# Pooled attention and a routed expert layer on one core: the next unit's kind is read during the first layer, the transposes' compares stand ahead of their waits, and the second expert's weights begin after the first unit's first layer

## The chip, the core and the metric

The kernel runs on one core of a Trainium2 chip. The metric is the device time of one execution in microseconds (us); lower is better. Engines are named as in the profile: PE is the matrix engine, PEld its weight loads, DVE the vector engine, ACT the scalar engine, POOL the gather and scatter engine, SP the engine that issues the weights' transfers. Each has a sequencer of its own that runs register loads, compares, branches and semaphore waits in program order and hands the other instructions to its engine. A "q" behind an engine's name (PEq, PEldq) is that sequencer.

## The reference, cut to what matters

```python
def reference(q, k, v, w_skip, w_gate, w1, w2):       # 8 x 8 heads, 576 tokens, 64 wide
    # attention: k and v averaged over 8 tokens, softmax(q k^T / 8) v
    x = attention(q, k, v)                            # 4608 tokens x 512
    out = x.copy()
    do = (x @ w_skip) > 0                             # tokens that get an expert
    xc = x[do]
    e_idx = argmax(xc @ w_gate); gate = softmax(xc @ w_gate)[e_idx]
    for e in range(8):
        m = e_idx == e
        y[m] = gate[m] * (relu(xc[m] @ w1[e]) @ w2[e])   # 512 -> 1024 -> 512
    out[do] = xc + y
```

## The kernel before, in words

The attention is written out flat and fills the first 165 us or so; the tokens' routes are computed beside it. From 184.4 us on runs the part that the change touches, `experts`: a loop whose trip count and kinds come from the data.

**Units.** The tokens of each expert are cut into units of up to three tiles of 128 rows, called places 0, 1 and 2. `nti` holds for each unit its kind (how many places, how wide the last one is), and `ends` (0: the expert goes on, 1 or 2: this is its last unit, 2 with a short last tile), and the count of units. Each engine runs its own copy of the loop over units (`units`, a `Fori`) and keeps `kind`, `ends` and `after` (the last unit's `ends`) in registers; at the end of a pass it loads the next unit's two values from `nti` (L1114, L1115).

**PE, in a unit.** `first`: 8 blocks f of 12 matmuls each (x, split in a high and a low part, by w1, split alike), into three PSUM tiles in turn; `by_width` chooses one of five copies of it by the unit's width (compares and branches at L1091). From f = 3 on it waits for `lo`, by which DVE tells that block f - 3 is evacuated. Then `second` for places 0 and 1 (24 matmuls each), `tx` (the next unit's rows, which POOL has gathered, are transposed, 4 matmuls a place), then place 2, as `second` or, where `ends` is 2, `second_short` (16 matmuls). Place 2 and place 0 share a PSUM tile: `P(t, "psf0")` waits until DVE has taken place 0's result out of it. At the head of `first` PE waits for `x` (the rows, transposed and split by ACT and DVE).

**ACT and DVE, in a unit.** For each block f ACT writes the high part of the hidden layer (L1355) and DVE the low part (L1413). After an `ends` unit they also split the next expert's weights: the four chunks of w2 within the first layer (at f = 1, 3, 5, 7), and behind the first layer of an `ends` unit the four chunks of the next w1 (ACT L1341, DVE L1390). Then DVE adds places 0 and 1 to their rows (L1398), makes the low part of the next rows (L1385, `x`), adds place 2 (L1398, or L1404 and L1409 for a short one), and its sequencer loads the next unit's values.

**Weights.** An expert's w1 and w2 come in 8 chunks of 512 KB into 8 staging buffers, issued by SP in order (L1149). The second expert's 8 chunks wait for the semaphore `first`, which PE raises for each unit and SP waits for once; each chunk of a later expert waits until DVE has split the chunk before it in its buffer. Each engine's program is itself brought in by transfers: the profile's queue named "instruction".

**POOL** scatters each place's results to the output when `ob0` to `ob2` are raised, gathers the rows of the unit after the next, and raises `land0` to `land2` as they land.

Of the kernel before, what the change touches and what calls it, by code (L numbers as in the profile page):

```python
# [44 lines left out]
UNITS = MAXU + 2  # L45
# [19 lines left out]
TWO = 1  # L65
# [992 lines left out]
    return got  # L1058


def registers(e, nti):
    regs = [e.alloc_register(n) for n in ("tot", "kind", "ends", "after")]
    e.reg_mov(regs[3], 0)
    yield regs
    for r, i in zip(regs, (2 * UNITS, 0, UNITS)):
        e.reg_load(r, nti[0:1, i:i + 1])
        yield regs


def experts(tc, nc, out, w1, w2, whi, wlo, slot, gate, nti, kinds_a, steps, near, bufs, mb, ident, psum, upper):  # L1070
# [5 lines left out]
    with tc.tile_critical(no_gpsimd_drain=True):  # L1076
# [4 lines left out]
        def P(e, n, by=1):  # L1081
            e.wait_ge(sem[n], by).then_inc(sem[n], -by)  # L1082

        def V(e, n, by=1):
            e.sem_inc(sem[n], by)
# [17 lines left out]
            return (lambda: e.snap(off, min_val=0, max_val=3 * RW),  # L1103
                    lambda: e.reg_alu(off, off, 3 * RW, ALU.bitwise_xor))

        def units(e, regs, body):

            tot, kind, ends, after = regs
            n = e.snap(tot, min_val=1, max_val=MAXU)
            with e.Fori(0, n) as u:  # L1110
                body(u, e.snap(kind, min_val=0, max_val=TWO + 4), e.snap(ends, min_val=0, max_val=2),
                     e.snap(after, min_val=0, max_val=2), n - u)
                e.reg_mov(after, ends)
                e.reg_load(kind, nti[0:1, bass.ds(u + 1, 1)])  # L1114
                e.reg_load(ends, nti[0:1, bass.ds(u + UNITS + 1, 1)])  # L1115

        def by_width(e, kind, go, marks=None):

# [18 lines left out]
        with nc.Block(no_gpsimd_drain=True) as blk:  # L1137
# [81 lines left out]
            def _(t):  # L1219
                at, turn = parity(t, 1)  # L1220
                
                def tx(u):

                    o, after = at(), held[3]
                    t.reg_load(after, nti[0:1, bass.ds(u + 1, 1)])
                    three = t.snap(after, min_val=0, max_val=TWO + 4)
                    for i in range(3):
                        P(t, f"land{i}")
                    for unit, this in ((0, o < 1), (1, o > 0)):
                        def place(i, n):  # L1230
                            for k in range(4):
                                m = t.transpose(psD[i][:, k * 128:k * 128 + 128],
                                                ring[:, 3 * unit + i, k * 128:k * 128 + 128], ident)
                            m.then_inc(sem["pe"], n)

                        with t.If(this):
                            with t.If(three > TWO):
                                place(0, 1)
                                place(1, 1)
                            with t.If(three < TWO + 1):  # L1240
                                place(1, 2)
                            place(2, 1)
                    turn()

                def first(xs):

                    P(t, "x")
                    V(t, "first")
                    for f in range(8):
                        if f > 2:  # L1250
                            P(t, "lo")
                        ps, w = psL[f % 3][:, xs], slice(f * 128, f * 128 + 128)
                        for k in range(4):
                            t.matmul(ps, whi[0][:, k, w], xhi[:, k, xs], start=(k == 0), stop=False)  # L1254
                            t.matmul(ps, whi[0][:, k, w], xlo[:, k, xs], start=False, stop=False)  # L1255
                            last = t.matmul(ps, wlo[0][:, k, w], xhi[:, k, xs], start=False, stop=(k == 3))  # L1256
                        last.then_inc(sem["pe"], 1)
# [20 lines left out]
                        last = t.matmul(ps, hlo[:, k, sl], whi[1][:, k, :], start=False, stop=(k == 7))  # L1278
                    last.then_inc(sem["l2"], 1)

                def unit(u, kind, ends, _, left):
                    by_width(t, kind, first, marks)
                    with t.If(kind > TWO):
                        second(0, True)
                        second(1, False)
                    with t.If(kind < TWO + 1):
                        with t.If(kind > TWO - 1):
                            second(1, True)
                    with t.If(left > 1):
                        tx(u)  # L1290
                    with t.If(kind < TWO):
                        for _ in range(3):
                            P(t, "lo")
                    P(t, "psf0")
                    with t.If(ends < 2):
                        second(2, False)
                    with t.If(ends > 1):
                        second_short()

                assert len(steps) == SPARE  # L1300
                loads = registers(t, nti)
                held = next(loads)
                marks = {}

# [11 lines left out]
                for n, (_, _, f) in enumerate(steps):  # L1316
# [8 lines left out]
                    if n in BETWEEN:  # L1325
# [2 lines left out]
                        for k in range(4):  # L1328
                            m = t.transpose(psD[i][:, k * 128:k * 128 + 128], ring[:, i, k * 128:k * 128 + 128], ident)
                        m.then_inc(sem["pe"], 1)  # L1330
                units(t, held, unit)

            def half(f):

                return 4 + f // 2 if f % 2 else None

            @blk.scalar
            def _(a):
                def split(c):
                    P(a, f"wd{c}", 16)  # L1340
                    a.activation(chunk_of(whi, c), chunk_view(stage[c], c), AF.Copy).then_inc(sem["whi"], 1)  # L1341

                def x_high(i):
                    P(a, "pe")
                    a.activation(xhi[:, :, i * 128:i * 128 + 128], psD[i].rearrange("p (k n) -> p k n", k=4),  # L1345
                                 AF.Copy).then_inc(sem["act"], 1)

                def unit(u, kind, ends, after, left):
                    def parts(xs):
                        for f in range(8):  # L1350
                            if f % 2:
                                with a.If(after > 0):
                                    split(half(f))
                            P(a, "pe")
                            a.activation(hhi[:, f, xs], psL[f % 3][:, xs], AF.Relu).then_inc(sem["act"], 1)  # L1355

                    by_width(a, kind, parts)
                    with a.If(left > 1):
                        with a.If(ends > 0):
                            for c in range(4):  # L1360
# [12 lines left out]
            def _(v):  # L1373
# [34 lines left out]
                    v.engine_nop().then_inc(sem["psf0"], 1)  # L1408
                    v.scalar_tensor_tensor(x, upper, rf[0:64, bass.ds(o + (2 * RW + D), 1)], x, ALU.mult, ALU.add).then_inc(sem["ob2"], 1)  # L1409

                def unit(u, kind, ends, after, left):
                    def low(out, f, xs):
                        return v.scalar_tensor_tensor(out[:, f, :], psL[f % 3][:, xs], 0.0, hhi[:, f, xs].bitcast(F32), ALU.max, ALU.subtract)  # L1413

                    def parts(xs, short):
                        for f in range(8):
                            if f % 2:
                                with v.If(after > 0):
                                    split(half(f))
                            P(v, "act")  # L1420
                            if short:
                                full, rest = slice(xs.start, 256), slice(256, min(xs.stop, 320))
# [103 lines left out]
```

## Time and profile before

| what | us |
|---|---|
| median of 3 runs (509.96 to 510.27) | 509.99 |
| the profiled execution, its own time | 508.82 |
| its span, from the first to the last instruction | 507.0 |
| PE busy in the span | 476.9 (94%) |
| DVE busy | 288.4 (57%) |
| ACT busy | 231.3 (46%) |
| POOL busy | 211.9 (42%) |

The span is the stretch of the profile in which the program's instructions run; the profiled execution took 1.8 us more than it. Busy time of PE is from modelled ends; for what PE loses, the starts of its matmuls are the better reading.

### The profile page before, as it was taken

What the parts mean: (1) busy time and instruction counts of PE and PEld (TensorE: products, weight loads), DVE (VectorE), ACT (ScalarE), POOL (GpSimd) and SP (SyncE); (2) the same over time, 40 slices, a digit from 0 to 9 for tenths busy, and PEclk for the clock granted to TensorE, in tenths of its full rate; (3) what the DMA queues carried; (4) which work ended last, traced back from release to release, by engine and by line L of the source; (5) the groups of instructions that cost most, each with busy time, mean ns of one, the idle gap of its engine ahead of it and who ended that gap; (6) DMA issues with size and microseconds to landing.
All of it is one profiled execution on the core that took longest, in us unless ns stands there. A gap on an engine that the chain in (4) does not pass through costs nothing. (4 is left out here: it accounts for less than half of the span.)

```text
span 507.0 us, 10450 instructions
## 1 busy us (share of the span) xinstructions
PE 476.9 (94%) x3175; PEld 431.7 (85%) x3176; DVE 288.4 (57%) x700; ACT 231.3 (46%) x583; POOL 211.9 (42%) x268
## 2 busy tenths in 40 slices
PE   7999999999969897999999998899999999999994
PEld 4799899988959687898989987889899898989893
DVE  5877887787747434457565738742536644232321
ACT  5677788888851024145444537521435342212110
POOL 5498599997544330233304023422022223223221
PEclk9999999999979899999999999999999999999998
DMA  8999999985111147548471646752325120101001
GB/s 286 398 392 394 349 360 333 356 307 168 65 44 45 37 139 293 191 142 263 158 263 54 194 158 219 250 176 61 103 112 166 62 70 33 62 21 59 29 13 39
DMA packets 33987, 87.02 MB, mean 172 GB/s; under 512 B 7278, under 2 KB 7406, under 8 KB 32288
## 3 DMA queue, kind: packets, MB, share of 16 engines
q1 hardware_dynamic: 26016, 71.62, 39.9%
q0 software_dynamic: 7936, 14.99, 9.0%
q8 instruction: 15, 0.25, 0.2%
q14 instruction: 20, 0.16, 0.1%
HBM read 73.25 MB, written 20.73 MB: 185 GB/s over the span
## 5 line engine op out<-in xcount | busy, mean ns | idle before, releaser
L1254 PE MATMUL psl<-xhi,w1hi 128*128 128x256 f32 (+3 forms) x384 | 112.9, 294 | 3.2 <-PEq L1082 2.2
L1256 PE MATMUL psl<-xhi,w1lo 128*128 128x256 f32 (+3 forms) x384 | 112.5, 293 | 0.0
L1255 PE MATMUL psl<-xlo,w1hi 128*128 128x256 f32 (+3 forms) x384 | 112.4, 293 | 0.0
L1169 POOL DMA_INDIRECT out<-ring,slot x36 | 37.2, 1033 | 164.9 <-POOLq L1082 159.0
L1355 ACT ACTIVATE hhi<-psl 128x256 fp32r<-128x256 f32 (+3 forms) x96 | 39.3, 410 | 119.4 <-ACTq L1082 116.2
L1413 DVE SCALAR_TENSOR_TENSOR hlo<-psl,hhi 128x256 fp32r<-128x256 f32 (+2 forms) x96 | 40.5, 423 | 66.2 <-DVEq L1082 61.1
L1254 PEld LDWEIGHTS psl<-xhi,w1hi 128*128 128x128 f32 x384 | 72.1, 188 | 5.0 <-issue 4.6
L1255 PEld LDWEIGHTS psl<-xlo,w1hi 128*128 128x128 f32 x384 | 72.1, 188 | 0.4
L1256 PEld LDWEIGHTS psl<-xhi,w1lo 128*128 128x128 f32 x384 | 72.1, 188 | 0.0
L297 ACT ACTIVATE e<-sc,mn 128x72 f32<-128x72 f32 x288 | 65.0, 345 | 7.4 <-DVE mn L291 6.9
L1345 ACT ACTIVATE xhi<-psd 128x512 fp32r<-128x512 f32 x36 | 19.1, 598 | 74.8 <-ACTq L1082 74.8
L323 PE MATMUL o<-vbd,pT 128*128 128x148 f32 (+1 forms) x312 | 50.4, 302 | 1.2 <-DVE x L342 1.2
L1164 POOL DMA_INDIRECT ring<-out,slot x39 | 40.9, 1049 | 20.1 <-issue 16.7
L397 POOL DMA_INDIRECT table<-pay,r_di x36 | 36.0, 1001 | 22.5 <-issue 6.8
L323 PEld LDWEIGHTS o<-vbd,pT 128*128 128x128 f32 (+1 forms) x312 | 39.4, 182 | 3.8 <-issue 1.1
L1276 PE MATMUL psf<-w2hi,hhi 128*128 128x512 f32 x96 | 38.0, 396 | 3.0 <-PEq L1082 3.0
L1390 DVE TENSOR_TENSOR w2lo<-stage,w2hi 128x1024 fp32r<-128x1024 f32 x28 | 34.2, 1223 | 8.6 <-DVEq L1082 7.5
L1277 PE MATMUL psf<-w2lo,hhi 128*128 128x512 f32 x96 | 37.4, 390 | 0.0
L1278 PE MATMUL psf<-w2hi,hlo 128*128 128x512 f32 x96 | 37.4, 390 | 0.0
L310 ACT ACTIVATE pT<-pt 128x640 f32<-128x640 f32 x36 | 25.5, 708 | 24.1 <-PE pt L306 15.2
L1163 POOL COPY ring<-gate 128x1 f32<-128x1 f32 x36 | 12.8, 357 | 54.1 <-DMA out<-ring,slot 47.5
L291 DVE TENSOR_REDUCE mn<-sc 128x4 f32<-128x288 f32 x72 | 30.6, 453 | 8.4 <-issue 3.7
(247 smaller groups left out, 989.7 us busy)
## 6 DMA issues: line engine op xcount, KB each, us to landing
stage<-in_w SPq DMA_DIRECT2D x64, 512.0 KB, 3.6
out<-x SPq DMA_DIRECT2D x36, 256.0 KB
stage<-in_k SPq DMA_DIRECT2D x6, 1152.0 KB
qt<-in_q SPq DMA_DIRECT2D x9, 512.0 KB
hhi<-in_vm SPq DMA_DIRECT2D x4, 1024.0 KB
hlo<-in_vm SPq DMA_DIRECT2D x3, 1024.0 KB
stage<-in_k SPq DMA_DIRECT2D x8, 288.0 KB
xhi<-in_q SPq DMA_DIRECT2D x4, 512.0 KB
```

The source lines that it names most:

```text
L297: nc.scalar.activation(ev[:, h // 2, k0:k0 + SP], sc[:, h * SP:(h + 1) * SP], AF.Exp, bias=mn[:, 4 * i + h:4 * i + h + 1], scale=-1.0)
L323: nc.tensor.matmul(o_[sl, g * 2 * VA:(g + 1) * 2 * VA], pT[:, 2 * a + g, sl], vbd[b % 2][:, 2 * a + g, :], start=(g == 0), stop=False)
L1164: g.indirect_dma_start(ring[:, s % 6, 0:D], None, out, bass.IndirectOffsetOnAxis(ap=slot[:, s:s + 1], axis=0), bounds_check=NTOK - 1, oob_ ...
L1169: g.indirect_dma_start(out, bass.IndirectOffsetOnAxis(ap=offsets, axis=0), ring[:, s % 6, 0:D], None, bounds_check=NTOK - 1, oob_is_err=Fa ...
L1254: t.matmul(ps, whi[0][:, k, w], xhi[:, k, xs], start=(k == 0), stop=False)
L1255: t.matmul(ps, whi[0][:, k, w], xlo[:, k, xs], start=False, stop=False)
L1256: last = t.matmul(ps, wlo[0][:, k, w], xhi[:, k, xs], start=False, stop=(k == 3))
L1276: t.matmul(ps, hhi[:, k, sl], whi[1][:, k, :], start=(k == 0), stop=False)
L1277: t.matmul(ps, hhi[:, k, sl], wlo[1][:, k, :], start=False, stop=False)
L1278: last = t.matmul(ps, hlo[:, k, sl], whi[1][:, k, :], start=False, stop=(k == 7))
L1355: a.activation(hhi[:, f, xs], psL[f % 3][:, xs], AF.Relu).then_inc(sem["act"], 1)
L1413: return v.scalar_tensor_tensor(out[:, f, :], psL[f % 3][:, xs], 0.0, hhi[:, f, xs].bitcast(F32), ALU.max, ALU.subtract)
```

## The change

PE's sequencer used to load the next unit's kind within `tx`; it now keeps it in a register a unit ahead (`later`), loaded at the end of a pass. ACT and DVE load the next unit's `kind` and `ends` into spare registers (`then`) ahead of block f = 2 of the first layer, and move them at the end of the pass. In `tx`, the three waits for landed rows, which stood together ahead of the compares, now stand each ahead of its own place's transposes. The raising of `first` stands behind `by_width` instead of at the head of `first`.

```diff
-def registers(e, nti):
+def registers(e, nti, n=3):
...
-    for r, i in zip(regs, (2 * UNITS, 0, UNITS)):
+    for r, i in zip(regs[:n], (2 * UNITS, 0, UNITS, 1)):
         e.reg_load(r, nti[0:1, i:i + 1])
...
-        def units(e, regs, body):
+        def units(e, regs, body, later=None):
...
+            if later is None:
+                then = [e.alloc_register(n_) for n_ in ("kind2", "ends2")]
...
+                def ahead():
+                    for r, i in zip(then, (1, UNITS + 1)):
+                        e.reg_load(r, nti[0:1, bass.ds(u + i, 1)])
...
-                e.reg_mov(after, ends)
-                e.reg_load(kind, nti[0:1, bass.ds(u + 1, 1)])
-                e.reg_load(ends, nti[0:1, bass.ds(u + UNITS + 1, 1)])
+                if later is None:
+                    e.reg_mov(after, ends)
+                    e.reg_mov(kind, then[0])
+                    e.reg_mov(ends, then[1])
+                else:
+                    e.reg_mov(kind, later)
+                    e.reg_load(later, nti[0:1, bass.ds(u + 2, 1)])
+                    e.reg_load(ends, nti[0:1, bass.ds(u + UNITS + 1, 1)])
...
-                def tx(u):
-
-                    o, after = at(), held[3]
-                    t.reg_load(after, nti[0:1, bass.ds(u + 1, 1)])
-                    three = t.snap(after, min_val=0, max_val=TWO + 4)
-                    for i in range(3):
-                        P(t, f"land{i}")
+                def tx(three):
+
+                    o = at()
                     for unit, this in ((0, o < 1), (1, o > 0)):
                         def place(i, n):
+                            for j in range(i + 1 - n, i + 1):
+                                P(t, f"land{j}")
...
                     P(t, "x")
-                    V(t, "first")
                     for f in range(8):
...
                     by_width(t, kind, first, marks)
+                    V(t, "first")
                     with t.If(kind > TWO):
...
                     with t.If(left > 1):
-                        tx(u)
+                        tx(t.snap(held[3], min_val=0, max_val=TWO + 4))
...
# in ACT's and in DVE's unit, in the loop over f:
+                            if f == 2:
+                                ahead()
```

At the end of a pass on DVE stand, before, two loads behind the last place's result (L1409; an ISA row is a register operation, and so is REGISTER_ALU):

```order
L1409 SCALAR_TENSOR_TENSOR ring<-upper,ring 64x512
L1457 UNCONDITIONAL_BRANCH
L1104 REGISTER_ALU
L1113 ISA
L1114 TENSOR_LOAD nti
L1115 ISA
L1115 TENSOR_LOAD nti
L1110 REGISTER_ALU
L1110 COMPARE_AND_BRANCH
```

and after, at the same place:

```order
L1422 SCALAR_TENSOR_TENSOR ring<-upper,ring 64x512
L1472 UNCONDITIONAL_BRANCH
L1104 REGISTER_ALU
L1122 ISA
L1114 COMPARE_AND_BRANCH
```

The two loads and two of the register rows are gone from there. They stand now in the first layer, here in DVE's copy for 256 columns, between blocks 1 and 2 (L1403 is the split of a chunk of w2, L1426 a block's low part):

```order
+L1426 SCALAR_TENSOR_TENSOR hlo<-psl_2525,hhi 128x256
+L1117 ISA
+L1117 TENSOR_LOAD nti
+L1117 ISA
+L1117 TENSOR_LOAD nti
+L1426 SCALAR_TENSOR_TENSOR hlo<-psl_2526,hhi 128x256
+L1431 COMPARE_AND_BRANCH
+L1403 TENSOR_TENSOR w2lo<-stage,w2hi 128x1024
```

They follow block 1's evacuation and the split ahead of it, and block 2's wait follows them.

On PE, `tx` ahead of the first transposes, before (in square brackets the semaphores that PE has waited for by that row):

```order
L1289 COMPARE_AND_BRANCH
L1103 ISA
L1225 TENSOR_LOAD nti
L1236 COMPARE_AND_BRANCH [waits m_land0,m_land1,m_land2]
L1237 COMPARE_AND_BRANCH
```

and after, at the same place and on into the transposes:

```order
L1301 ISA
L1247 COMPARE_AND_BRANCH
L1248 COMPARE_AND_BRANCH
L1243 MATMUL psd0_2527<-cfs_69,ring_580 128x128 [waits m_land0]
L1243 MATMUL psd0_2527<-cfs_69,ring_580 128x128 x3
L1243 MATMUL psd1_2528<-cfs_69,ring_580 128x128 [waits m_land1]
L1243 MATMUL psd1_2528<-cfs_69,ring_580 128x128 x3
```

The load is gone from `tx`, and each wait moved from the head of `tx` to its own transposes, behind the compares. The raising of `first` is an instruction of the sequencer alone, which this listing doesn't show; the diff above tells where it stands.

## Rows read from the trace of the kernel before

**Rows 1.** What PE waited for in the expert stage, 184 to 501 us, the two longest lines: us in total, times, longest us.

```profile
PE psf L1276 <- PEq L1082: 3.0, 1, 3.0
PE psl L1254 <- PEq L1082: 2.2, 2, 1.8
```

**Rows 2.** The timeline of PE at the end of unit 1's first layer: start, length, what, and in brackets the idle time before it.

```profile
198.29 0.31 PE L1255 MATMUL psl<-xlo,w1hi 128*128 128x320 f32 x1
198.43 0.31 PE L1256 MATMUL psl<-xhi,w1lo 128*128 128x320 f32 x1
201.73 0.47 PE L1276 MATMUL psf<-w2hi,hhi 128*128 128x512 f32 x1 [2.99 <-PEq L1082]
```

**Rows 3.** Branches of `by_width` on PE's sequencer, each asked for alone: count, shortest, median and longest in ns, and when. In order: the one that ends unit 1's first layer, the one that enters it, and the one that ends unit 2's first layer.

```profile
L1091 PEldq COMPARE_BRANCH  x1: 5461/5461/5461, 196.0 to 196.0; - x1
L1091 PEldq COMPARE_BRANCH  x1: 2656/2656/2656, 181.3 to 181.3; - x1
L1091 PEldq COMPARE_BRANCH  x1: 233/233/233, 227.2 to 227.2; - x1
```

**Rows 4.** Transfers by queue (packets, MB, share of 16 engines) in four windows in turn: 181.6 to 181.7; 198.9 to 199.1; 195.9 to 198.9, in which no packet of an instruction queue stands; and 194 to 195.9 us. q8 is an instruction queue, q1 the weights'.

```profile
q8 instruction: 1, 0.02, 59.9%
...
q8 instruction: 1, 0.02, 36.1%
...
q1 hardware_dynamic: 461, 0.89, 80.2%
...
q1 hardware_dynamic: 391, 0.76, 105.4%
```

**Rows 5.** Three places where PE stops ahead of f = 3 of a first layer, in units 2, 4 and 5: its timeline.

```profile
221.34 0.28 PE L1256 MATMUL psl<-xhi,w1lo 128*128 128x256 f32 x1
222.09 0.35 PE L1254 MATMUL psl<-xhi,w1hi 128*128 128x256 f32 x1 [0.47 <-issue]
...
275.31 0.31 PE L1256 MATMUL psl<-xhi,w1lo 128*128 128x320 f32 x1
275.68 0.39 PE L1254 MATMUL psl<-xhi,w1hi 128*128 128x320 f32 x1
...
304.09 0.28 PE L1256 MATMUL psl<-xhi,w1lo 128*128 128x256 f32 x1
304.87 0.36 PE L1254 MATMUL psl<-xhi,w1hi 128*128 128x256 f32 x1 [0.51 <-issue]
```

**Rows 6.** DVE ahead of the first of them: the first evacuation of unit 2, then the loads of its sequencer at the end of unit 1's pass, with the register operation behind them (ns, when).

```profile
221.51 0.42 DVE L1413 SCALAR_TENSOR_TENSOR hlo<-psl,hhi 128x256 fp32r<-128x256 f32 x1 [1.48 <-DVEq L1082]
...
L1114 DVEq TENSOR_LOAD <-nti x1: 329/329/329, 219.5 to 219.5; - x1
...
L1115 DVEq TENSOR_LOAD <-nti x1: 317/317/317, 220.0 to 220.0; - x1
...
L1110 DVEq ALU_OP  x1: 49/49/49, 220.3 to 220.3; - x1
```

**Rows 7.** The end of unit 5, which has only a short place 2: PE's timeline; DVE's (w1's splits, then the next rows); and on PE's sequencer the wait for `psf0` and the raising of `first` (ns, when).

```profile
311.95 0.28 PE L1256 MATMUL psl<-xhi,w1lo 128*128 128x256 f32 x1
313.84 1.08 PE L1232 MATMUL psd<-cfs,ring 128*128 128x128 f32 x8 [1.61 <-PEq L1082]
315.14 0.49 PE L1262 MATMUL psf<-w2hi,hhi 128*128 128x512 f32 x1 [0.21 <-issue]
...
320.82 0.36 PE L1254 MATMUL psl<-xhi,w1hi 128*128 128x256 f32 x1 [1.77 <-PEq L1082]
...
314.09 4.63 DVE L1390 TENSOR_TENSOR w1lo<-stage,w1hi 128x1024 fp32r<-128x1024 f32 x4
318.64 1.88 DVE L1385 TENSOR_TENSOR xlo<-psd,xhi 128x512 fp32r<-128x512 f32 x3
...
L1082 PEldq EVENT_SEMAPHORE  x1: 51/51/51, 314.6 to 314.6; - x1
...
L1085 PEldq EVENT_SEMAPHORE  x1: 51/51/51, 320.7 to 320.7; - x1
```

**Rows 8.** The weights. In order: PE raises `first` (ns, when); SP's issues of the second expert's chunks and of the third's first four (start of the first); MB that queue q1 had moved from 184.8 us to 193.3 and to 200.3 us, and from 201.9, when the third expert's first four chunks were issued, to 210 us; SP's issues in 184 to 215 us with the time from issue to landing, which is that of the second expert's last chunk, issued at 189.94.

```profile
L1085 PEldq EVENT_SEMAPHORE  x1: 51/51/51, 184.3 to 184.3; - x1
...
184.87 20.80 SPq L1149 DMA_DIRECT2D stage<-in_w  x12
...
q1 hardware_dynamic: 580, 2.10, 76.2%
...
q1 hardware_dynamic: 1658, 4.18, 77.9%
...
q1 hardware_dynamic: 565, 2.06, 77.0%
...
stage<-in_w SPq DMA_DIRECT2D x12, 512.0 KB, 11.3
```

**Rows 9.** Unit 1 behind its first layer, timelines: ACT splits w1; DVE takes place 0's result; PE works on the short place 2 and begins unit 2.

```profile
199.34 3.91 ACT L1341 ACTIVATE w1hi<-stage 128x1024 fp32r<-128x1024 f32 x4
...
207.76 0.75 DVE L1398 SCALAR_TENSOR_TENSOR ring<-psf,ring 128x512 f32 x1 [2.58 <-DVEq L1082]
...
213.53 0.48 PE L1262 MATMUL psf<-w2hi,hhi 128*128 128x512 f32 x1
...
217.26 0.28 PE L1254 MATMUL psl<-xhi,w1hi 128*128 128x256 f32 x1
```

More of the change, by code (lines that the diff above doesn't have):

```diff
@@ L1104, in parity @@
                     lambda: e.reg_alu(off, off, 3 * RW, ALU.bitwise_xor))
-        def units(e, regs, body):
+        def units(e, regs, body, later=None):
             tot, kind, ends, after = regs
             n = e.snap(tot, min_val=1, max_val=MAXU)
+            if later is None:
+                then = [e.alloc_register(n_) for n_ in ("kind2", "ends2")]
+                for r in then:
+                    e.reg_mov(r, 0)
             with e.Fori(0, n) as u:
+                def ahead():
+                    for r, i in zip(then, (1, UNITS + 1)):
+                        e.reg_load(r, nti[0:1, bass.ds(u + i, 1)])
                 body(u, e.snap(kind, min_val=0, max_val=TWO + 4), e.snap(ends, min_val=0, max_val=2),
-                     e.snap(after, min_val=0, max_val=2), n - u)
-                e.reg_mov(after, ends)
-                e.reg_load(kind, nti[0:1, bass.ds(u + 1, 1)])
-                e.reg_load(ends, nti[0:1, bass.ds(u + UNITS + 1, 1)])
+                     e.snap(after, min_val=0, max_val=2), n - u, ahead)
+                if later is None:
[6 more added lines that the diff above has]
+                    e.reg_load(ends, nti[0:1, bass.ds(u + UNITS + 1, 1)])
         def by_width(e, kind, go, marks=None):
@@ L1279, in second, with unit @@
                     last.then_inc(sem["l2"], 1)
-                def unit(u, kind, ends, _, left):
+                def unit(u, kind, ends, _, left, ahead):
                     by_width(t, kind, first, marks)
+                    V(t, "first")
                     with t.If(kind > TWO):
@@ L1300, in _ @@
                 assert len(steps) == SPARE
-                loads = registers(t, nti)
+                loads = registers(t, nti, 4)
                 held = next(loads)
@@ L1330, in _ @@
                         m.then_inc(sem["pe"], 1)
-                units(t, held, unit)
+                units(t, held, unit, held[3])
             def half(f):
@@ L1346, in x_high, with unit @@
                                  AF.Copy).then_inc(sem["act"], 1)
-                def unit(u, kind, ends, after, left):
+                def unit(u, kind, ends, after, left, ahead):
                     def parts(xs):
@@ L1409, in result_short, with unit @@
                     v.scalar_tensor_tensor(x, upper, rf[0:64, bass.ds(o + (2 * RW + D), 1)], x, ALU.mult, ALU.add).then_inc(sem["ob2"], 1)
-                def unit(u, kind, ends, after, left):
+                def unit(u, kind, ends, after, left, ahead):
                     def low(out, f, xs):
@@ L1419, in parts @@
                                     split(half(f))
+                            if f == 2:
+                                ahead()
                             P(v, "act")
```

## The prediction

> **What bounds the kernel now.** I read the waits first: over the whole expert stage PE's longest wait is a single one of 3.0 us ahead of a second layer, and the next line adds 2.2 us ahead of first layers [rows 1]. So PE sets the pace from 184 us to the end, and whatever it stops waiting for comes off the time, if nothing else takes its place. As matmul ends are modelled, I read its stops as the distance between two starts, less the usual step: 0.12 us for 256 columns, 0.14 for 320.
>
> Then the timeline at each stop. In unit 1, PE starts its last first-layer matmul at 198.43 and the next matmul at 201.73 [rows 2]: 3.30 - 0.14 = 3.16 us lost. What stood in the way is a branch of the sequencer: it leaves the first layer at 196.0 and takes 5.46 us; the same branch at the end of unit 2 takes 0.23 [rows 3]. The branch that enters the first layer takes 2.66 and has its instruction packet on the move from 181.6, 0.3 us after it began; the slow one began at 196.0, and no instruction packet moved until 198.9 [rows 3, 4]. In between, the second expert's weights filled the queues: from 194 to 195.9 they took more than all of the 16 engines' time [rows 4]. I read this as a load of code that waits for the weights.
>
> Three smaller stops stand ahead of f = 3, in units 2, 4 and 5: 222.09 - 221.34 - 0.12 = 0.63, 0.37 - 0.14 = 0.23, and 0.78 - 0.12 = 0.66 [rows 5]. At each PE waits for DVE's first evacuation, which starts late because DVE's sequencer has the two loads at the end of the pass to do: 0.33 and 0.32 us, and from the first's start at 219.5 to the next operation at 220.3 some 0.8, with DVE idle for 1.48 us ahead of the evacuation [rows 6]. Last, unit 5 ends with two stops, 311.95 to 313.84 and 2 us ahead of 320.82; the latter ends right behind DVE's w1 splits and next rows, 314.09 to 320.52 without a break [rows 7].
>
> **The change, part by part.**
>
> *a. `first` leaves the head of the first layer.* Where PE waited for `x`, its raising stood between that wait and the first matmul: 184.2 or 184.3 in unit 1, 320.7 ahead of 320.82 in unit 5's end [rows 7, 8]. About 0.1 us each: 0.2 gained. In the other units the sequencer reaches that place ahead of its engine, as it also reaches the new one (the branch of unit 2 begins at 227.2, 0.23 long, without a stop [rows 3]), so there it costs nothing; without that cover it would be 0.1 a unit.
>
> *b. The weights no longer stand in the way of unit 1's branch.* The trace has no such branch in this place without traffic. Bounds: at best 0.23 long, as once its code is there, and all 3.16 us come back; at worst 5.46 as now, and nothing does. I take the entering branch, 2.66, nearest in kind: a first visit, with quiet queues. It ends 2.80 earlier, less 0.1 for `first` behind it: 2.7 gained, and PE still waits some 0.4.
>
> *c. The second expert's weights come later.* PE raises `first` at about 201.4 - 2.8 - 0.1 = 198.5; SP's first issue came 0.55 after it (184.3, 184.87 [rows 8]), so 199.1 instead of 184.87. Who waits: ACT for the chunks, behind it DVE's splits of w1, behind these, in DVE's order, place 0's result, and for that PE's short place 2, through `psf0`. Four chunks are 2.10 MB; they had moved 8.4 us after the first issue for the second expert, and after 8.1 for the third, all but 0.04 MB [rows 8]. A landing is told up to 0.9 later: the last chunk landed at 189.94 + 11.3 = 201.2, and 4.18 MB had moved by 200.3 [rows 8]. So w1 is there between 207.2 and 208.4. Then one split on ACT (0.98 of its four in 3.91), one on DVE (1.16 of four in 4.63), the result (0.75), and from `psf0` to the first matmul 0.5 (314.6, 315.14) [rows 7, 9], with three hand-overs of 0.1 (estimate): 3.7. The short place 2 starts at 210.9 to 212.1; PE would be there at 213.53 - 2.8 = 210.7 [rows 9]. Cost 0.2 to 1.4; I take 0.9, as the issue in one go resembles the second expert's case, less the 0.26 MB that gathers moved in it. What is late next is `x` for unit 2: place 1's result and three tiles of next rows, 0.75 + 1.88 [rows 7], are 2.7 us behind `psf0`, while place 2 lasts 217.26 - 213.53 = 3.7 [rows 9]: hidden. The w2 chunks land in the next 7 us, as their splits begin in unit 2. The place-0 scatter on POOL starts 2.6 us later and has a whole unit of cover.
>
> *d. DVE's loads leave the end of the pass.* Two loads and their address work, 0.8 us, against one register row: the first evacuation comes 0.75 earlier, which is more than each of the three stops (0.63, 0.23, 0.66). All 1.52 us come back. In unit 5 the whole run of ACT and DVE up to 320.52 hangs on that start, and so moves with it; the stop there stays, 0.66 earlier. ACT's loads gate no stop of PE.
>
> *e. The loads at f = 2.* They take 0.8 us of ACT's and of DVE's sequencer between two evacuations that are 12 x 0.12 = 1.4 apart: no cost. On DVE a split of 1.16 on the engine covers them where there is one. If they did delay block 2, PE needs it only three blocks later.
>
> *f. `tx`.* Its load and the order of waits and compares matter where PE stands and waits for rows, unit 5 alone: up to 0.9 of the 1.8 us before 313.84. But the next stop, at 320.82, is set by DVE, so place 2 ends earlier and PE waits longer: nothing. PE's extra load at the start lies ahead of queued matmuls: nothing, at most its 0.33.
>
> Sum: a 0.2, b 2.7, c -0.9, d 1.5: 3.5 us faster. The profiled execution took 508.82, so 505.3 of its own; the runs' median is 1.2 higher, 509.99, and 506.5 by that. A measurement of this kernel can tell about 0.2%, 1.0 us, from no change.
>
> **The rivals.**
>
> *1. The load of code is only partly the weights' fault.* One engine carries 391 packets / 16 in 1.9 us, so a packet of 2 KB takes 0.08 us [rows 4]; if the load waits for some 16 of these and is slow for another reason, 1.3 us come back instead of 2.7: 2.1 faster, 507.9. For it: the packet came only 2.9 us after the branch. Against: it came when the weights thinned out. [...]
>
> *2. The branch doesn't care about the weights.* Then b is nothing, `first` comes at 201.4, c stays 0.9, as PE is late by as much: 0.2 - 0.1 - 0.9 + 1.5 = 0.7 faster, 509.3, no change to be told. Against: the entering branch's 2.66, and the 0.3 us to its packet.
>
> *3. The weights come later than their earlier loads did*, by 2 us more, in a queue shared with unit 1's scatters: c is 2.9, 1.5 faster, 508.5.
>
> *4. Slower: place 2 of unit 1 stands long behind w1.* Without c the gains are 4.4; to lose 1.0, c must be 5.4, so the short place starts at 216.1, and w1 lands at 212.4, 13.3 us after the first issue. That is 2.10 MB at 158 GB/s, against 8.4 to 9.3 us seen. For it: nothing hides any later landing.
>
> **How the numbers follow.** My forecast 0.62, around 506.5 (505.7 to 507.2 by c's bounds); rival 1 0.13; rival 2 0.10; rival 3 0.07; rival 4 0.05; and 0.03 for more than forecast: c at nothing and b at 3.16, 4.9 faster, 505.1. The range reaches from there to rival 3: 505.0 to 508.4. Faster by over 0.2%: 0.62 + 0.13 + 0.07 + 0.03 = 0.85; within: 0.10; slower: 0.05.
>
> **What would show it.** b: the branch ends near 198.5 after some 2.7 us, its instruction packet moves within 0.5 us of its start, and the gap of 3.3 in [rows 2] shrinks to about 0.6. c: a new wait of PE ahead of the short place 2 of unit 1, 0.2 to 1.4 long, with DVE's place-0 result right behind the fourth w1 split. d: no step over 0.2 us ahead of f = 3 in units 2, 4, 5. f: transposes of unit 5 begin earlier, 320.82's stop stays. Wrong it would be if the branch still took over 4 us, or if w1's fourth chunk landed later than 209.

## The result: 0.8% slower, and the profile of the changed kernel

The changed kernel takes 514.18 us (median of five runs, 512.55 to 515.54) against 509.99 for the kernel before (509.21 to 510.9 beside it): a ratio of 1.0082, 95% interval 1.0053 to 1.0110. It is 4.2 us slower where 3.5 us of gain were forecast. The profiled execution took 512.55 us, its span is 510.8. Every ratio here and in the experiments below leaves out the runs over 1.5% above the fastest of their kernel, of which the kernel before has one (920.55 us), the kernel called "third expert held" two of twelve, and "result of place 0 between" four of twelve (503.61 to 505.52 us); over all twelve runs the medians of the last two are 502.7 and 501.8 us, against 502.2 for the kernel before beside either.

What PE waited for in the expert stage of the changed kernel, 184 to 502 us (us in total, times, longest), to be set against [rows 1]:

```profile
PE psd L1243 <- PEq L1082: 5.5, 4, 2.3
PE psf L1286 <- PEq L1082: 1.3, 1, 1.3
PE psl L1264 <- PEq L1082: 1.2, 1, 1.2
PE psf L1272 <- issue: 0.3, 1, 0.3
```

The longest wait of before, 3.0 us at the branch out of unit 1's first layer, is now 1.3 (`psf`, L1286). At the top stands a group that had one wait of 1.6 before: the transposes of `tx`, which wait for rows that POOL has gathered. Where they lie is seen in the lengths of the units, from a unit's first matmul to the next one's (us, worked out from PE's timelines):

| unit | 1 | 2 | 3 | 4 | 5 | 6 |
|---|---|---|---|---|---|---|
| before | 32.83 | 24.27 | 28.65 | 29.83 | 20.81 | 23.64 |
| changed | 31.46 | **30.41** | 28.65 | 29.55 | 20.09 | 23.47 |

Units 1 and 4 to 6 gained 2.5 us; unit 2 lost 6.1. PE's timeline there (start, length, what, in brackets the idle time ahead), from the `tx` of unit 2 on:

```profile
232.68 0.60 PE L1243 MATMUL psd<-cfs,ring 128*128 128x128 f32 x4
234.47 0.63 PE L1243 MATMUL psd<-cfs,ring 128*128 128x128 f32 x4 [1.19 <-PEq L1082]
...
237.42 1.09 PE L1243 MATMUL psd<-cfs,ring 128*128 128x128 f32 x4 [2.32 <-PEq L1082]
238.42 0.79 PE L1286 MATMUL psf<-w2hi,hhi 128*128 128x512 f32 x1
239.00 0.63 PE L1287 MATMUL psf<-w2lo,hhi 128*128 128x512 f32 x1
239.43 0.63 PE L1288 MATMUL psf<-w2hi,hlo 128*128 128x512 f32 x1
...
243.69 0.40 PE L1286 MATMUL psf<-w2hi,hhi 128*128 128x512 f32 x1
243.92 0.40 PE L1287 MATMUL psf<-w2lo,hhi 128*128 128x512 f32 x1
```

PE stands ahead of place 1's transposes and of place 2's, 4.2 us with the small pieces. Behind that, matmuls stand 0.43 us apart, and 0.23 again from 243.69 on. The reason is the clock: the window from 236.8 to 243.6 us (PEclk is the eighth entry: us, then busy time and instructions of five engines, the granted clock, DMA share, GB/s):

```profile
236.80:243.60 6.80, 6.18 (x16) 4.89 (x17) 0.69 (x1) 0.60 (x1) 3.22 (x4) 0.50 0.42 150
```

The granted clock is 0.50 there, and 1.00 in the window behind it, 243.7 to 246 us. The twelve matmuls from 238.42 to 243.69 take 5.27 us instead of 12 x 0.23: 2.5 lost. Stops and clock together, 6.7 us, less the 0.78 that the step ahead of f = 3 gave back in this unit, make 5.9 of the 6.1.

Why the rows are late is seen on POOL. Its timeline before (L1169 scatters, L1164 gathers), from the scatter of unit 1's place 0 to the two gathers that unit 2's `tx` needs:

```profile
209.44 1.03 POOL L1169 DMA_INDIRECT out<-ring,slot  x1 [15.63 <-POOLq L1082]
212.82 0.18 POOL L1163 COPY ring<-gate 128x1 f32<-128x1 f32 x1 [2.35 <-DMA out<-ring,slot]
213.56 1.05 POOL L1164 DMA_INDIRECT ring<-out,slot  x1 [0.57 <-issue]
214.95 1.02 POOL L1169 DMA_INDIRECT out<-ring,slot  x1 [0.34 <-issue]
220.94 0.98 POOL L1169 DMA_INDIRECT out<-ring,slot  x1 [4.97 <-POOLq L1082]
...
225.07 1.07 POOL L1164 DMA_INDIRECT ring<-out,slot  x1 [0.16 <-POOL ring L1163]
...
226.50 1.03 POOL L1164 DMA_INDIRECT ring<-out,slot  x1 [0.16 <-issue]
```

and of the changed kernel (L1182 scatters, L1177 gathers):

```profile
212.58 1.03 POOL L1182 DMA_INDIRECT out<-ring,slot  x1 [22.81 <-POOLq L1082]
219.04 0.18 POOL L1176 COPY ring<-gate 128x1 f32<-128x1 f32 x1 [5.44 <-DMA out<-ring,slot]
219.79 2.09 POOL L1177 DMA_INDIRECT ring<-out,slot  x1 [0.57 <-POOLq L1082]
222.18 1.91 POOL L1182 DMA_INDIRECT out<-ring,slot  x1 [0.30 <-issue]
224.40 0.99 POOL L1182 DMA_INDIRECT out<-ring,slot  x1 [0.31 <-issue]
...
229.01 1.06 POOL L1177 DMA_INDIRECT ring<-out,slot  x1 [0.16 <-issue]
...
230.67 1.83 POOL L1177 DMA_INDIRECT ring<-out,slot  x1 [0.16 <-issue]
```

POOL does everything in one order: scatter place 0, wait until it has landed, gather into its rows, scatter places 1 and 2, wait until these have landed, gather the other two. The first scatter starts 3.1 us later, where 2.6 were forecast, and then takes 6.4 us to land instead of 3.3. Two of POOL's own issues behind it take longer too, 2.09 and 1.91 us instead of 1.05 and 1.02, for which no run shows a cause. So place 2's scatter, which used to wait for its data (4.97 us idle), now comes 3.5 us later than before, of which those two issues make 1.9; and the gathers come 4 us later, while PE is there 2 us earlier. What moved in the queues while the first scatter was on its way (q1 the weights, q0 POOL's), from 212.6 to 216.8 us and from 216.8 to 219 in the changed kernel:

```profile
q1 hardware_dynamic: 514, 1.72, 103.6%
...
q1 hardware_dynamic: 137, 0.48, 53.7%
q0 software_dynamic: 80, 0.26, 29.6%
```

For 4.2 us not one of the scatter's 80 packets moves; they go when the weights thin out. These are the last chunks of the second expert and the first of the third, which now run in one piece from 201.5 to 218.5 us. In the kernel before, all 80 moved between 211 and 212.8 beside five packets of weights.

### The profile page after: what moved, and what is told of

Its sections match the earlier page's. It is cut to its first block, busy times and chain, and to the rows that moved or that the text cites. A ratio compares the mean times of both kernels' runs of the same rounds, so it can differ in the third digit from the quotient of the medians.

```text
span 510.8 us, 10433 instructions
## 1 busy us (share of the span) xinstructions
PE 479.5 (94%) x3175; PEld 433.8 (85%) x3176; DVE 289.0 (57%) x700; ACT 231.2 (45%) x583; POOL 213.3 (42%) x268
## 5 line engine op out<-in xcount | busy, mean ns | idle before, releaser
L1182 POOL DMA_INDIRECT out<-ring,slot x36 | 39.3, 1091 | 166.1 <-POOLq L1082 159.9
L1426 DVE SCALAR_TENSOR_TENSOR hlo<-psl,hhi 128x256 fp32r<-128x256 f32 (+2 forms) x96 | 40.3, 422 | 61.8 <-DVEq L1082 59.2
L1177 POOL DMA_INDIRECT ring<-out,slot x39 | 42.6, 1093 | 21.5 <-issue 16.4
L1286 PE MATMUL psf<-w2hi,hhi 128*128 128x512 f32 x96 | 39.1, 407 | 1.3 <-PEq L1082 1.3
L1403 DVE TENSOR_TENSOR w2lo<-stage,w2hi 128x1024 fp32r<-128x1024 f32 x28 | 34.4, 1228 | 10.2 <-DVEq L1082 9.1
L1403 DVE TENSOR_TENSOR w1lo<-stage,w1hi 128x1024 fp32r<-128x1024 f32 x28 | 32.7, 1220 | 7.6 <-DVEq L1082 7.3
```

Source lines behind the costliest of these rows:

```text
L1177: g.indirect_dma_start(ring[:, s % 6, 0:D], None, out, bass.IndirectOffsetOnAxis(ap=slot[:, s:s + 1], axis=0), bounds_check=NTOK - 1, oob_ ...
L1182: g.indirect_dma_start(out, bass.IndirectOffsetOnAxis(ap=offsets, axis=0), ring[:, s % 6, 0:D], None, bounds_check=NTOK - 1, oob_is_err=Fa ...
L1286: t.matmul(ps, hhi[:, k, sl], whi[1][:, k, :], start=(k == 0), stop=False)
L1403: v.tensor_tensor(chunk_of(wlo, c), chunk_view(stage[c], c), chunk_of(whi, c).bitcast(F32), ALU.subtract).then_inc(sem["wlo"], 1)
```

## The experiments

They ran on several chips, and on some of them the part ahead of the experts ends 5 to 10 us earlier; so times are given as a ratio to the kernel before on the same chip, and places in a trace by the distance from the start of unit 2's first matmul. Two tables hold the measurements.

| kernel | ratio to before | 95% interval |
|---|---|---|
| before, again | 1.0004 | 0.9977 to 1.0031 |
| changed, again | 1.0070 | 1.0051 to 1.0088 |
| `first` moved alone | 1.0076 | 1.0047 to 1.0105 |
| changed, `first` at the head | 0.9983 | 0.9954 to 1.0012 |
| reads ahead alone | 0.9999 | 0.9974 to 1.0024 |
| changed, third expert held | 0.9987 | 0.9953 to 1.0020 |
| changed, result of place 0 between | 0.9943 | 0.9908 to 0.9978 |
| changed, gather behind the scatters | 0.9946 | 0.9919 to 0.9973 |
| before, scatter late | 0.9996 | 0.9964 to 1.0027 |
| before, scatter last | 1.0215 | 1.0178 to 1.0253 |
| weights parted, alone | 0.9926 | 0.9902 to 0.9950 |
| changed, weights parted | **0.9907** | 0.9887 to 0.9926 |

From one trace of each: POOL's issues in us from unit 2's start (the scatters of unit 1's places 0 and 2, and the gather into place 1's rows), how long place 0's scatter took to land, the stops in unit 2's `tx`, the stop at unit 1's branch and the one ahead of its short place 2.

| trace | scatter 0 | landing | scatter 2 | gather 1 | stops in `tx` | branch | short place 2 |
|---|---|---|---|---|---|---|---|
| before | -7.8 | 3.3 | 3.7 | 7.8 | 0 | 3.15 | 0 |
| before, again | -7.8 | 2.8 | 3.7 | 7.8 | 0 | 3.61 | 0 |
| changed | -3.4 | 6.4 | 8.4 | 13.0 | 4.2 | 1.42 | 0.28 |
| changed, again | -3.4 | 6.1 | 6.2 | 13.0 | 3.9 | 1.64 | 1.60 |
| `first` moved alone | -5.0 | 5.9 | 4.3 | 7.8 | 0 | 1.29 | 2.73 |
| third held | -5.0 | 2.8 | 3.7 | 10.2 | 0 | 1.18 | 2.10 |
| result between | -5.7 | 6.8 | 4.6 | 10.3 | 0 | 1.17 | 0 |
| gather behind | -5.0 | 6.3 | 3.7 | 7.4 | 0 | 1.52 | 2.08 |
| scatter late | -2.3 | 2.8 | 4.0 | 7.8 | 0 | 2.93 | 0 |
| scatter last | 3.7 | 2.8 | 10.5 | 16.2 | 8.3 | 3.07 | 0 |
| weights parted (changed) | -7.8 | 5.6 | 3.7 | 7.4 | 0 | 1.36 | 0 |

**Which part of the change is it?** `first` back at the head of the changed kernel, and moved alone in the kernel before:

```diff
 # changed, first at the head               # before, first moved alone
     P(t, "x")                                  P(t, "x")
+    V(t, "first")                         -    V(t, "first")
...
     by_width(t, kind, first, marks)            by_width(t, kind, first, marks)
-    V(t, "first")                         +    V(t, "first")
```

> The changed kernel with the raising of `first` back at the head of the first layer; the reads ahead and the order of `tx` stay. Theory (the later weights delay POOL's scatter of unit 1's place 0 and all that POOL does behind it): the weights move from 185 again, the scatter takes about 3.3 us instead of 6.4, `tx` of unit 2 has no wait over 0.5 us, and TensorE's granted clock stays full in units 2 and 5. Unit 1's branch is back at about 5.4 us. Against the kernel before only the three stops ahead of f = 3 go (1.5 us): 508.4. Rival A (the waits for landed rows, each ahead of its own transposes, cost it, by letting PE stand in small pieces): stops and a low clock in the `tx` of unit 2 stay, 512 to 514. Rival B (the loads within the first layer delay ACT and DVE): also 512 to 514, with new stops in the first layers.

> The kernel before with the raising of `first` moved behind the first layer, and nothing else of the change. Theory: everything of the loss is in this part: unit 1's branch gains 1.7 us, `tx` of unit 2 waits some 4 us for rows and loses some 2.6 more at the low clock, unit 5 loses some 2; the stops ahead of f = 3 stay (1.5). About 515.5. Rivals A and B: the branch's 1.7 us less 0.3 at the short place 2, so 508.5.

The loss goes with `first`: moved alone it costs 3.8 us (0.76% of 502), without it the changed kernel is no slower. Rivals A and B fall. The profiled execution of `first` moved alone, 502.56 us, is the fastest of its eight; the median is 506.58. Its trace shows another price of the later weights than the first trace of the changed kernel: no stop in unit 2's `tx`, but 2.73 us ahead of unit 1's short place 2, PE's timeline

```profile
202.03 0.60 PE L1232 MATMUL psd<-cfs,ring 128*128 128x128 f32 x4
205.20 0.49 PE L1261 MATMUL psf<-w2hi,hhi 128*128 128x512 f32 x1 [2.56 <-PEq L1082]
```

and a granted clock of 0.5 for 3.4 us behind it: unit 1 takes 35.38 us there, 2.5 more than in the first trace of before. Where the slower seven executions lose, no trace shows.

**The same two kernels again, for a trace of both on one more chip.**

> The kernel before, once more, for a trace on this chip and to see by how much the same kernel differs from itself: a ratio of 1.000 within 0.003. Its expert stage should again lose some 3 us at unit 1's branch, and have no low clock in unit 2.

> The changed kernel, once more. Its ratio should again be about 1.008. Theory E (two prices of the later weights, of which a run pays one or the other: either w1 lands soon, the short place 2 of unit 1 hardly waits, and POOL's late chain stops `tx` of unit 2; or w1 lands 2 us later, and the short place 2 itself stands 2 to 2.8 us, as in the two runs with the later weights so far, and the low clock follows there): either 2 to 3 us ahead of the short place 2, or 3 to 4 us in `tx` of unit 2, and a stretch of low clock right behind it. Rival C' (only POOL's chain counts): again stops in `tx` of unit 2.

Neither theory had it right: the second trace of the changed kernel pays both, 1.60 us ahead of the short place 2, and in unit 2 again

```profile
224.01 0.60 PE L1243 MATMUL psd<-cfs,ring 128*128 128x128 f32 x4
225.87 0.63 PE L1243 MATMUL psd<-cfs,ring 128*128 128x128 f32 x4 [1.25 <-PEq L1082]
228.48 1.08 PE L1243 MATMUL psd<-cfs,ring 128*128 128x128 f32 x4 [1.98 <-PEq L1082]
```

with the low clock from 227.7 for 6.8 us: unit 2 took 30.03 us, as in the first trace. POOL's chain is late by another link as well: place 2's scatter itself now takes 5.87 us to land, where it took 2.53 before. POOL's timeline:

```profile
213.50 1.90 POOL L1182 DMA_INDIRECT out<-ring,slot  x1 [0.30 <-issue]
219.60 0.58 POOL L1176 COPY ring<-gate 128x1 f32<-128x1 f32 x1 [4.21 <-DMA out<-ring,slot]
```

The kernel before, again, has a surprise of its own (last section).

**Is it the traffic or the late result?** In one kernel the third expert's weights wait for the scatter of place 0; in the other, the kernel before, that scatter waits for place 1's result:

```diff
 # changed, third expert held
             s.wait_ge(sem["wlo"], 8 * (i - 2) + c + 1)
+        if i == 2 and c == 0:
+            s.wait_ge(sem["sc0"], 32)
 # before, scatter late
+    if u == 0:
+        g.wait_ge(sem["ob1"], 1)
     P(g, "ob0")
     scatter(slot[:, s:s + 1], s)
```

> The changed kernel, with the third expert's weights held back until the scatter of unit 1's place 0 has landed. Theory (the weights in the queues stretch the scatter): only the second expert's last chunks, which land by 215.4, still stand beside it, so it lands at about 216 instead of 219; POOL's chain moves up by about 3 us, the two long waits of unit 2's `tx` (3.8 us together) shrink to about 1, the clock stays full there, and unit 5's shrink too: 508.5 to 510.5. Rival C (place 0's result comes 3 us later from DVE, since it stands behind the w1 splits, and that alone delays POOL): the scatter lands at 218 to 219 and the time stays at 513 to 514.

> The kernel before, in which POOL holds the scatter of unit 1's place 0 until place 1's result is there too: it starts at about 214.9 instead of 209.44, in queues with no weights in them, and should land at about 218.2, some 0.8 us ahead of the changed kernel's 218.98. Theory (what counts is when that scatter lands, whether traffic or a late result holds it, as POOL does its gathers and scatters one behind the other): `tx` of unit 2 waits about as in the changed kernel, with a low clock behind it: 509.99 + 5 to 8 = 515 to 518. Rival D (the gathers themselves are slowed by weights, and the scatter's landing doesn't matter): under 511.

With the third expert held, POOL's timeline is

```profile
206.41 1.03 POOL L1184 DMA_INDIRECT out<-ring,slot  x1 [24.33 <-POOLq L1082]
209.24 0.18 POOL L1178 COPY ring<-gate 128x1 f32<-128x1 f32 x1 [1.81 <-DMA out<-ring,slot]
...
215.14 0.98 POOL L1184 DMA_INDIRECT out<-ring,slot  x1 [2.80 <-POOLq L1082]
```

The scatter of place 0 lands in 2.8 us, the stops in `tx` go, and so does the loss (0.9987), though the short place 2 costs 2.10. Rival C falls. The other run corrected my theory: 5.5 us of lateness cost nothing. At -2.3 the scatter goes even later than in the changed kernel (-3.4), but lands in 2.8 us, and place 2's scatter then stands at 4.0, as its data are only there at 3.7. Lateness alone is covered; lateness and a landing of 6 us are not.

**How far does the cover reach?** The same hold, until place 2's result:

```diff
+    if u == 0:
+        g.wait_ge(sem["ob2"], 1)
     P(g, "ob0")
```

> The kernel before, in which POOL holds the scatter of unit 1's place 0 until place 2's result is there, some 11 us late (about 214 instead of 203), with no second or third expert's w1 in its way. Theory (POOL's chain has a slack of some 5 us ahead of unit 2's `tx`, and what delays it by more is paid, whatever the cause): scatter 214, gather and the other scatters behind it, landed about 223, gathers 224.5 and 226, landed about 229 and 231, against rows wanted at 227.8: `tx` of unit 2 stops 2 to 4 us in all, and the low clock may follow; ratio 1.004 to 1.010. Rival H (only the weights' traffic at the scatter counts): no stop there, ratio 1.000.

```profile
234.45 0.39 PE L1280 MATMUL mb<-w2hi,hlo 128*128 128x512 f32 x1
242.94 2.81 PE L1234 MATMUL psd<-cfs,ring 128*128 128x128 f32 x12 [8.09 <-PEq L1082]
```

PE's timeline of that run: one stop of 8.1 us ahead of the transposes, a low clock from within it (0.5 from 237.4 for 10.2 us), and 2.15% in time. I had expected 0.4 to 1%: the gathers, now at 16.2 and 18.1, took up to 7.2 us to land; at that distance, 233.5 to 242 us, the next weights took 76.7% of the engines' time in the first trace of before. Rival H falls: a late chain is paid though the scatter itself lands in 2.8 us. Set side by side, the traces give the cover: with place 1's gather at 7.4 to 10.3 us behind unit 2's start PE doesn't stop, at 13.0 it loses 4, at 16.2 over 8.

**Is POOL's order a link of the chain?** The gather into place 0's rows goes behind the scatters of places 1 and 2; or DVE takes place 0's result after two of the four w1 splits:

```diff
 # changed, gather behind the scatters
     P(g, "ob0")
     scatter(slot[:, s:s + 1], s)
-    if u + 1 < MAXU:
-        with g.If(tot > u + 1):
-            done("sc0", 16)
-            gather(s + 6)
     for i in (1, 2):
         P(g, f"ob{i}")
         scatter(slot[:, s + i:s + i + 1], s + i)
+    if u + 1 < MAXU:
+        with g.If(tot > u + 1):
+            done("sc0", 16)
+            gather(s + 6)
 # changed, result of place 0 between (the conditions around the splits left out)
-    for c in range(4):
-        split(c)
-    with v.If(kind > TWO):
-        result(0)
+    split(0); split(1)
+    with v.If(kind > TWO):
+        result(0)
+    split(2); split(3)
```

> The changed kernel, in which POOL issues the scatters of places 1 and 2 ahead of waiting for the scatter of place 0 and gathering into its rows. Theory (POOL's order: the scatter of place 2, whose rows are there at about 210, waits until 213.5 behind the stretched scatter of place 0 and the gather): that scatter goes at about 211, lands by 214, and the gathers for `tx` of unit 2 go 3 us or more earlier: no stop over 0.5 us there and no low clock behind it. The short place 2 of unit 1 still waits 1.6 to 2.7. Ratio 0.998 to 1.002. Rival H (the gathers are slow whenever weights move, and POOL's order is nothing): stops of 2 us or more stay in `tx` of unit 2, ratio 1.005 to 1.008.

> The changed kernel, in which DVE takes place 0's result after two of the four w1 splits instead of after all of them, in each unit that ends an expert. Theory E: the short place 2 of unit 1 no longer waits for w1's last chunks, and the scatter of place 0 is issued some 3 us earlier, though still among the weights: of the loss of 0.8% at least half goes, ratio 1.000 to 1.004, unless unit 2's `tx` still stops. Rival C' (the traffic alone counts, whenever the result is there): the scatter still takes about 6 us and `tx` of unit 2 still stops 3 us: 1.006 to 1.008.

POOL with the gather behind:

```profile
212.91 1.02 POOL L1182 DMA_INDIRECT out<-ring,slot  x1 [24.61 <-POOLq L1082]
214.24 0.98 POOL L1182 DMA_INDIRECT out<-ring,slot  x1 [0.31 <-issue]
221.61 0.97 POOL L1182 DMA_INDIRECT out<-ring,slot  x1 [6.39 <-POOLq L1082]
...
223.11 1.06 POOL L1177 DMA_INDIRECT ring<-out,slot  x1 [0.16 <-issue]
```

The landing is as slow as ever (6.3 us), but place 2's scatter waits for its data again (6.39 idle, at 3.7 of unit 2), the gathers go at 7.4, and unit 2 is back to 23.47 us. In the second the scatter starts 2.3 us earlier and takes 6.8; that is enough. Both kernels are clearly faster than the changed one: 0.9946 against 1.0082 or 1.0070, and for the second 501.8 us over all its runs against 505.95 on the same chip. By their ratios both are also some 0.5% faster than the kernel before, more than I expected. Where that comes from is not shown: from unit 1's first matmul to the end the trace with the gather behind takes 322.8 us, the first trace of before 322.6; and the second kernel is level with before over all its runs (501.8 against 502.2). Rivals H and C' fall. So neither the traffic nor the time of the result alone is the cause, but their sum, through POOL's order.

**The reads ahead by themselves** (the changed kernel with `first` at the head and the old order in `tx`):

> The kernel before with only the reads ahead (ACT's and DVE's loads at block 2, PE's register); `tx` and `first` as before. It is the forecast's step d by itself: the stops ahead of f = 3 (0.62, 0.2 and 0.66 us in the last trace of before) are gone, 1.5 us, ratio 0.997. Rival G (what is gained there is given back at the next stop, in unit 5, or by the low clock): the three stops are gone, the stop of unit 5 grows, ratio 0.999 to 1.001.

Rival G came nearer. Unit 2 is 0.78 us shorter and unit 4 0.26, as forecast, but unit 5 isn't:

```profile
313.00 0.28 PE L1267 MATMUL psl<-xhi,w1lo 128*128 128x256 f32 x1
316.97 1.96 PE L1243 MATMUL psd<-cfs,ring 128*128 128x128 f32 x8 [3.70 <-PEq L1082]
```

The step ahead of f = 3 is gone, and PE waits 3.70 us for gathered rows instead of 1.61 [rows 7]. Over all traces unit 5 takes 20.8 us on average in kernels with the reads ahead and in those without. The time, 0.9999, doesn't tell the remaining 1.0 us from nothing. The order in `tx` by itself had no run; the two kernels that differ by it alone (0.9983 and 0.9999) agree within their intervals.

**A version that beats both: the weights parted.** `first` is raised at both places, and SP sends five chunks of the second expert (w1 and one of w2) on the first, three on the second:

```diff
     if i > 1:
         s.wait_ge(sem["wlo"], 8 * (i - 2) + c + 1)
+    elif c == 5:
+        s.wait_ge(sem["first"], 2)
```

> The changed kernel, in which `first` is raised at both places: SP issues the first five chunks of the second expert (all of w1, one of w2) at the head of the first layer, and the other three behind it. Theory: w1 is there at about 195 as in the kernel before, so neither the short place 2 of unit 1 nor POOL's scatter meets it; the branch out of unit 1's first layer meets hardly any weights, so it loses 1.4 us or less instead of 3.1. With the stops ahead of f = 3 gone: 1.7 + 1.5 = 3.2 us faster than the kernel before, ratio 0.994. Rival F (the branch's load of code is slowed by what is still queued, or by something else than weights): the branch loses some 3 us as before, ratio 0.997. Rival A (the order in `tx` costs): 1.003 or more.

> The kernel before with only the weights parted: five chunks at the head of unit 1's first layer, three behind it. Theory: the branch's part alone, 3.6 - 1.4 = 2.2 us by the traces of the kernel before and of the parted weights on this chip, ratio 0.9955; with the reads ahead (0.997) it should give the 0.991 of the two together, or some 1 us less. Rival G: here too less than half of it, 0.998 or more.

```profile
192.93 0.31 PE L1269 MATMUL psl<-xhi,w1lo 128*128 128x320 f32 x1
194.43 0.47 PE L1289 MATMUL psf<-w2hi,hhi 128*128 128x512 f32 x1 [1.20 <-PEq L1082]
```

With nothing in the queues from 193 to 194.5 us (DMA share 0.00) PE stands 1.2 us at the branch (0.93% faster with the whole change; 0.74% alone). Rivals F, A and G fall. The scatter of place 0 still takes 5.6 us, but starts at -7.8 as before, so nothing is lost to it. The gain is larger than the 2.2 us of the branch. Behind its 3 us stop some traces with `first` at the head have a low clock, behind 1.7 us or less none has (last section); that may be the rest, but no run shows it apart. The lengths of the traces from unit 1's first matmul to the end would fit it: 319.6 us with the whole change and 321.1 with the weights parted alone, against 322.6 in the first trace of before, which has no low clock in unit 1, and 326.0 in the second, which has one.

## Why the prediction was wrong

- **The step that failed** is one sentence in c: "The place-0 scatter on POOL starts 2.6 us later and has a whole unit of cover." It starts 3.1 later; but the cover was counted from its start with its old length, and not along POOL's chain, where a landing, three issues, another landing and two gathers follow. The weights' new time, 201.5 to 218.5, lay beside it, and no term asked what they would do to it. The kernel before had the price. POOL's timeline there, under the second expert's weights:

```profile
185.84 0.99 POOL L1169 DMA_INDIRECT out<-ring,nslot  x1 [3.10 <-POOLq L1082]
...
191.99 0.18 POOL L1163 COPY ring<-gate 128x1 f32<-128x1 f32 x1 [3.74 <-DMA out<-ring,nslot]
```

  A scatter issued at 185.84 was waited for until 191.99: 6.1 us, against the 3.3 of the scatter at 209.44: the 3 us that the changed kernel lost at first hand. None of the rivals was this. The slower one sought the loss at the short place 2 and asked 5.4 us of it.
- **The clock** was not in the sum at all. A stop was priced at its length; the stops in unit 2 brought 2.5 us more.
- **b** had the right mechanism and the wrong size. The branch lasts 3.58 us:

```profile
L1091 PEldq COMPARE_BRANCH  x1: 3580/3580/3580, 196.1 to 196.1; - x1
```

  instead of 5.46 [rows 3], not 2.66 as its entering twin: 1.7 came back in the first trace (3.15 to 1.42), where 2.7 were forecast. Its instruction packet, the only packet of any queue from 196.1 to 199.7 us, moved 1.0 us after its start, not within 0.5. What such a packet carries no run shows; the branch ended 2.5 us behind it, as in the kernel before (198.9 [rows 4] and 196.0 + 5.46). Rival 2 falls. Rival 1 was half right: with the weights parted the branch still lasts 3.5 us and loses 1.4, so the weights were to blame for 1.7 of 3.15 us only. For how many packets of the weights a load waits no run shows: the 16 of rival 1 were an assumption, its 1.3 us an estimate from them, and 1.7 came back.
- **c** at the short place 2 was forecast at 0.9 (0.2 to 1.4) and measured at 0.28, 1.60, 2.73, 2.10 and 2.08 in the five traces in which the weights are later and place 0's result still stands behind all four splits: w1's fourth chunk landed 8.2 to 10.6 us after the first issue, where I allowed 8.1 to 9.3. The three hand-overs of 0.1 in its sum were an estimate without a row; in the first trace of the changed kernel DVE's result of place 0 ends at 211.65 and PE's wait for it at 211.7. Rival 3 had this half right.
- **d**: all three stops are gone as forecast, but only units 2 and 4 (1.0 us) keep the gain; in unit 5 rows from POOL set the end, which step f had seen for `tx`, but d had not.
- **a, e and f** cost and brought nothing that shows; unit 1 began 0.1 us later, not earlier.

The sum by the traces: b 1.7, d 1.0, c -0.3 to -1.6, unit 2 -6.7 (stops 4.2, clock 2.5, as in the first trace): 4.3 to 5.6 slower, against a measured 4.2 (2.7 to 5.6).

## What to carry to other kernels

When a large transfer is moved, list every small transfer of other engines that will now lie beside it, price each at its length under full traffic (here the old trace had one, 6.1 us against 3.3), and follow the engine that waits for it to the end of its chain before calling it covered. Part a burst rather than move it: what is needed first goes first, and the rest where nobody waits (here 0.9907 against 1.0082 for the move). And a stop of PE may cost more than its length: the 4.2 us in unit 2 brought 2.5 more at a granted clock of 0.50.

## What the runs showed of the hardware

- **A scatter under weights.** With q1 at 103.6% of the 16 engines (changed, 212.6 to 216.8 us), the first packet of POOL's scatter moved 4.3 us after its issue, against 1.6 in the first trace of before, with q1 at 23.1% until then, and in that of scatter late, with no packet of q1: 2.7 us more. In the seven traces in which the weights took over half of the engines' time until that scatter landed (60.1% in the changed kernel with the weights parted, 94.2% with the result of place 0 between), its first packet moved 2.4 to 4.4 us after its issue, and it landed after 5.2 to 6.8.
- **The clock after a stop.** In the eighteen stops of over 1 us at unit 1's branch and short place 2, in the traces above and in those of `first` at the head and the two single parts, the granted clock fell to 0.5 within 1.5 us of the end of six, each over 2 us long (2.08 with the gather behind, 2.10 with the third expert held, 2.47 with `first` at the head, 2.73 with `first` moved alone, 3.31 with the reads alone, 3.61 in before, again), and stayed there 3.4 or 6.8 us. Behind the stops of 1.7 us or less it didn't; behind three of about 3 us it didn't either (3.15 in before, 2.93 in scatter late, 3.07 in scatter last). In unit 5, where PE waits for rows, it fell in eleven of the fourteen traces (0.51 from 318.7 to 322.2 us in the first of the changed kernel, where PE stood 0.29, 1.72 and 0.34 us), and with `first` at the head behind three idle times of only 0.67, 0.80 and 0.65 us within 4 us. So the length of one stop doesn't decide it, and what does stays open. The kernel before pays it too, in its second trace, from 191.7 us:

```profile
191.70:198.40 6.70, 5.87 (x14) 4.64 (x15) 3.83 (x4) 1.89 (x2) 0.00 (x0) 0.50 0.70 224
```
